# Attention and two feed-forward layers on one core: the second layer's weights converted after the attention, with three pair buffers and a new table of durations

## The chip, the core and the metric

The kernel runs on one core of a Trainium2 chip. The metric is the device time of one execution, in microseconds (us). Six queues work side by side: TensorE (PE) multiplies matrices, VectorE (DVE) and ScalarE (ACT) work on elements, GpSimd (POOL) does so more slowly, SyncE (SP) issues all transfers, and sixteen DMA engines move the data. Each queue runs its instructions strictly in the order in which they were written.

## The reference

Four batches of eight heads attend over 576 positions with a head size of 64, with a learned relative bias. The result goes through two feed-forward layers of width 2048 over 2304 tokens.

```python
scores = scale * np.matmul(q, k.transpose(0, 1, 3, 2))
h = np.maximum((psi_rel / psi_i)[..., None] @ w1 + b1, 0.0)
scores = scores + (h @ w2).transpose(2, 0, 1)[None]
attn = np.exp(scores - scores.max(-1, keepdims=True))
attn = attn / (attn.sum(-1, keepdims=True) + 1e-09)
x = heads_joined(np.matmul(attn, v))          # (2304, 512)
r = np.maximum(x @ w_in, 0.0)                 # first layer
x = (s * (r * r) + b) @ w_out
h = x @ moe2_w_in                             # second layer
return (h - np.tanh(h)) @ moe2_w_out
```

The attention's inputs are float32, and the four weight matrices of the layers are float64.

## The kernel before

**Precision.** Every operand of a matmul is held as a pair of float16 numbers, a high part and a low part that is what the high part left over. A product takes three matmuls (high by high, high by low, low by high). So the kernel spends much of DVE, ACT and POOL on making pairs: `copy_scale` makes the high part (DVE or ACT), `low_part` the low part (DVE). A float64 weight is first made float32 by three DVE instructions on its bits, `conv_steps` (L906, L909, L912), and squares of it are summed on ACT for the scale of the pair.

**Attention.** There are 144 units, each for 128 rows of scores of one head (or of two heads with 64 rows). A unit runs: scores on PE into `sp` (L747, four matmuls), bias and maximum on DVE (L761), exponential on ACT into `e` (L771), its high part into the pair buffer `hl` on ACT or DVE (L782, L780), its low part on POOL (L788), a DMA transposition of `hl` into `et` (L794), and the weighted sum on PE into `xp` (L807, L814, fourteen matmuls). Rings of buffers limit how many units are under way: two of `sp`, two of `e`, two of `hl`, four of `et`, four of the bias `bi`. Ahead of them the bias is computed in 36 steps: a hidden layer `hid` (L456 on DVE or L460 on ACT, four instructions a step), a matmul, and a copy to the DRAM tensor `btd`, from which each unit loads its rows.

**First layer.** Whenever 256 tokens have all their heads, a block of it can run: 192 matmuls into `ph` (L1203), relu and square on ACT, high part on DVE (L1226), low part on POOL (L1230), 192 matmuls into `po` (L1270), and a store to the DRAM tensor `x2d`. Nine blocks make 3456 matmuls of 256 columns. The inputs of the blocks lie in a ring `xt` of two.

**Second layer.** Five blocks of tokens run `pg` (L1499), tanh and difference, and `pq` (L1546), 960 matmuls each, nearly all of 512 columns. Its weights are 8 tiles of 128 by 2048. While the attention runs, `w2_tasks` brings each in four quarters through two staging places in `w1big`: load of 512 KB float64, three DVE steps of 512 columns, a square on ACT (L1324), and a store of the float32 values to the DRAM tensor `w2d`. When all squares are summed and the scale is known, tiles 0 and 1 are loaded again and split into pairs during the attention's end. The task `turn` then gives up the attention's memory, and tiles 2 to 7 are loaded from `w2d` (`w2x`) and split.

**Order.** The order on every queue is not written out. Each step is a task with a duration for each engine that may run it, dependencies, a priority, and the buffers that it takes. A planner (`Schedule.forward`) goes through time, starts at each moment the task of least priority value that could start, and writes the instructions in that order. So the durations and the constants at the head of the file decide the order of all queues and which of two engines gets a task.

Of the kernel before, what the change touches and what calls it, by code (L numbers as in the profile page):

```python
# [11 lines left out]
U32 = mybir.dt.uint32  # L12
# [13 lines left out]
SHARE0, QP, QA, SCU = 0, 9, 15, 29  # L26
T0, R0, T1, RU = 46.51, 2.21, 135.37, 2.75
QL0, QLEAD, QSTEP = 12.97, -15.94, 0.15
WI0, WI1, WO0, WO1 = 33.65, 103.52, 57.73, 120.8
W2A, W2B, W2U, W2V = 467.42, 815.12, 71, 7  # L30
AHEAD = 1.46
# [138 lines left out]
def tile_kernel(  # L170
# [36 lines left out]
    xt_p = ctx.enter_context(tc.tile_pool(name="xt", bufs=2))  # L207
# [96 lines left out]
    w2d32 = dram.tile([128, 8, 2048], F32, name="w2d32")  # L304
# [10 lines left out]
    ROWS = dict(bi=4, e=2, hl=2, et=4)  # L315
    hr = wp.tile([128, 8 * 2 * S], F16, name="hr")
# [129 lines left out]
    def hid(Q, t, eng):  # L446
        if Q < QA:
            i = (Q % 2) * 4 + t
            h = hr[:, i * 2 * S:(i + 1) * 2 * S].bitcast(F32)
# [5 lines left out]
        if eng == DVE:  # L455
# [16 lines left out]
    def bias_tasks(Q):  # L472
# [3 lines left out]
        for t in range(4):  # L476
# [3 lines left out]
            else:  # L480
# [3 lines left out]
                {DVE: 0.48, ACT: 0.70}, lambda e, Q=Q, t=t: hid(Q, t, e), deps, d, [hid_i[Q, t]] if Q >= QA else []  # L484
# [5 lines left out]
        if Q < QP:  # L490
# [6 lines left out]
            t_bmm[Q].append(sc.add({PE: 1.2}, mm, hs, d - 1000, [i], hi))  # L497
# [3 lines left out]
            t_ev.append(sc.add({ACT: 0.65, DVE: 0.70}, out, t_bmm[Q], d, [ev], [i]))  # L501
        else:
            for hf in range(2):
# [4 lines left out]
                t_bmm[Q].append(sc.add({PE: 0.6}, mm, hs + t_bmm[Q], d - 1000, [i], hi))  # L508
# [927 lines left out]
    for n in range(32):  # L1436
        w2_tasks(n)
# [203 lines left out]
```

## Time and profile before

| | us |
|---|---|
| three timed runs | 1154.21, 1153.5, 1149.24 |
| their median | 1153.5 |
| the profiled execution | 1156.14 |
| its span, first to last instruction | 1154.3 |

The span is 1.84 us shorter than the time of the same execution. In the profile a line such as L1203 is a line of the kernel before. "Busy" is the union of an engine's instruction times. Matmuls overlap each other, so a busy PE may still be slower than it could be. PEclk is the granted TensorE clock as a share of 2.4 GHz, and the DMA share is the mean busy share of the sixteen engines; overlapping packets can lift it above 1.

### The profile page before, as it was taken

The numbers are of one execution on the slowest core, as the hardware profiler recorded it, in microseconds if no ns is written. First come the engines' busy times: TensorE is split into PE (matmuls) and PEld (weight loads), VectorE is DVE, ScalarE is ACT, GpSimd is POOL, SyncE is SP. The second block draws the span as 40 slices with busy tenths as digits, with TensorE's granted clock in tenths as the row PEclk, the third lists the DMA queues.
The fourth block names the chain that finished last, engine by engine and source line by source line (L and its number), as shares of the span: only waits on it lengthen the run. The fifth ranks groups of instructions, "written<-read, shape, count | busy, mean of one in ns | idle before, by whom it ended". The sixth has DMA issues, their size and how long they took to land.

```text
span 1154.3 us, 23401 instructions
## 1 busy us (share of the span) xinstructions
PE 1031.2 (89%) x9024; PEld 696.4 (60%) x9024; DVE 804.6 (70%) x1704; ACT 575.1 (50%) x1114; POOL 330.4 (29%) x364
## 2 busy tenths in 40 slices
PE   4466589999988888989888899999999999999998
PEld 2233267776777677877777778888554444444443
DVE  7999999787666897888878764787755444344320
ACT  7987877776688674655546553342211111111110
POOL 0043255455454374554635443210000000000000
PEclk9566778999999899999999999999999999999999
DMA  9997884997999989999999993550001000000000
GB/s 337 321 294 172 245 227 94 199 202 172 219 247 234 257 189 243 243 228 231 225 209 243 205 187 82 177 198 31 21 10 46 10 19 10 19 10 10 19 19 27
DMA packets 268736, 176.96 MB, mean 153 GB/s; under 512 B 200528, under 2 KB 227792, under 8 KB 267856
## 3 DMA queue, kind: packets, MB, share of 16 engines
q1 hardware_dynamic: 268624, 175.47, 61.5%
q8 instruction: 70, 1.15, 0.4%
q14 instruction: 42, 0.34, 0.1%
HBM read 99.79 MB, written 28.44 MB: 111 GB/s over the span
## 4 chain that ended last, share of the span: by engine, by line
PE 54%; DMA 14%; DVE 12%; ACT 4%; issue 3%; POOL 1%; SPq 1%; DVEq 0%; ACTq 0%; POOLq 0%
PE pq L1546 16%; PE pg L1499 16%; DMA et<-hl 11%; PE po L1270 8%; PE ph L1203 6%; PE sp L747 3%; DVE sp L761 2%; PE pb L464 2%; PE xp L807 2%; POOL hl L788 1%; PE xp L814 1%; DVE w1big L909 1%; DVE hr L1226 1%; ACT e L771 1%; DVE w1big L912 1%
## 5 line engine op out<-in xcount | busy, mean ns | idle before, releaser
L788 POOL TENSOR_TENSOR hl<-e,hl 128x64 f16<-128x64 f32 (+1 forms) x288 | 236.3, 842 | 318.5 <-ACT hl L782 216.7
L1270 PE MATMUL po<-hr,w1big 128*128 128x256 f16 x1728 | 209.3, 277 | 7.3 <-DVE x L1284 3.8
L1203 PE MATMUL ph<-xt,w1big 128*128 128x256 f16 x1728 | 205.7, 275 | 0.2 <-DVE p2a L228 0.2
L1270 PEld LDWEIGHTS <-w1big 128*128 128x128 f16 x1728 | 168.2, 100 | 37.6 <-issue 8.3
L1203 PEld LDWEIGHTS <-w1big 128*128 128x128 f16 x1728 | 166.9, 99 | 27.9 <-issue 5.8
L1507 ACT ACTIVATE t<-pg,ich 128x512 f32<-128x512 f32 (+1 forms) x80 | 51.6, 645 | 243.8 <-PE pg L1499 243.8
L1511 DVE SCALAR_TENSOR_TENSOR t<-pg,ich,t 128x512 f32<-128x512 f32 (+1 forms) x80 | 55.7, 696 | 153.3 <-ACT t L1507 153.3
L1546 PEld LDWEIGHTS <-w2big 128*128 128x128 f16 x960 | 93.9, 98 | 94.2
L771 ACT ACTIVATE e<-sp,mx 128x576 f32<-128x576 f32 x144 | 105.6, 734 | 64.4 <-POOL hl L788 56.7
L761 DVE CUSTOM_DVE_ANT_0 sp<-sp,bi 128x576 f32<-128x576 f32 x144 | 109.4, 760 | 31.4 <-PE sp L747 20.0
L1546 PE MATMUL pq<-w1big,w2big 128*128 128x512 f16 x576 | 130.8, 379 | 0.0
L1230 POOL TENSOR_TENSOR hr<-r,hr 128x512 f16<-128x512 f32 x72 | 94.9, 1318 | 110.8 <-DVE hr L1226 95.7
L747 PE MATMUL sp<-ks,qs 128*128 128x288 f16 (+1 forms) x640 | 102.6, 303 | 26.5 <-ACT e L771 26.3
L807 PE MATMUL xp<-vp,et 128*128 128x64 f16 (+1 forms) x1440 | 66.1, 199 | 36.3 <-DMA et<-hl 33.2
L807 PEld LDWEIGHTS <-et 128*128 128x128 f16 (+1 forms) x1440 | 56.1, 104 | 61.3 <-DMA et<-hl 50.2
L1499 PE MATMUL pg<-hr,w2big 128*128 128x512 f16 x384 | 88.1, 379 | 0.0
L747 PEld LDWEIGHTS <-qs 128*128 128x128 f16 (+1 forms) x640 | 54.6, 104 | 52.2 <-issue 38.6
L1499 PE MATMUL pg<-hr,w1big 128*128 128x512 f16 x384 | 85.7, 379 | 0.0
L782 ACT ACTIVATE hl<-e 128x576 f16<-128x576 f32 x89 | 60.2, 679 | 41.5 <-DMA et<-hl 36.1
L1499 PEld LDWEIGHTS <-w1big 128*128 128x128 f16 x480 | 47.0, 98 | 45.9
L1499 PEld LDWEIGHTS <-w2big 128*128 128x128 f16 x480 | 46.9, 98 | 44.7
L1546 PE MATMUL pq<-w2big 128*128 128x256 f16 (+1 forms) x384 | 66.0, 326 | 0.0
(155 smaller groups left out, 1356.3 us busy)
## 6 DMA issues: line engine op xcount, KB each, us to landing
bi<-btd SPq DMA_DIRECT2D x72, 288.0 KB, 4.3
btd<-et SPq DMA_DIRECT2D x36, 288.0 KB, 3.6
qst<-in_qd SPq DMA_DIRECT2D x36, 256.0 KB, 4.7
w1big<-in_win SPq DMA_DIRECT2D x8, 1024.0 KB, 7.8
w1big<-in_wout SPq DMA_DIRECT2D x8, 1024.0 KB, 6.5
w1big<-in_win SPq DMA_DIRECT2D x16, 512.0 KB, 4.9
w2d<-w1big SPq DMA_DIRECT2D x32, 256.0 KB, 3.4
w1big<-in_wout SPq DMA_DIRECT2D x16, 512.0 KB, 5.3
```

The source lines that it names most:

```text
L747: nc.tensor.matmul(out=s_[r0:r0 + r, hf, 0:HS], lhsT=qs.tile[:, s, c * r:c * r + r], rhs=ks.tile[:, a, hf * HS:(hf + 1) * HS], start=s == ...
L761: nc.vector.tensor_tensor_reduce(out=st, in0=st, in1=bi.tile.rearrange("p (a b) -> p a b", a=2), scale=-1.0 / KAP, scalar=3.0e38, op0=ALU. ...
L771: nc.scalar.activation(out=put(e, row_tile("e")).rearrange("p (a b) -> p a b", a=2), in_=sp.tile[:, :, 0:HS], func=AF.Exp, scale=-1.0, bia ...
L782: nc.scalar.activation(out=h[:, 0:S], in_=e.tile, func=AF.Copy)
L788: nc.gpsimd.tensor_tensor(out=hl.tile[:, o:o + m], in0=e.tile[:, c:c + m], in1=hl.tile[:, c:c + m], op=ALU.subtract)
L807: nc.tensor.matmul(out=xp[r0:r0 + r, col:col + 64], lhsT=et.tile[:, n, r0:r0 + r], rhs=vp.tile[:, 0, n % 5, 64 * a:64 * a + 64], start=n = ...
L1203: nc.tensor.matmul(out=ph.tile[:, fi, :], lhsT=win_ap(1, sw, m, f), rhs=xa(sx, m), start=m == 0 and j == 0, stop=m == KM - 1 and j == 2,)
L1230: nc.gpsimd.tensor_tensor(out=rh[:, :, 1, :], in0=r.tile, in1=rh[:, :, 0, :], op=ALU.subtract)
L1270: nc.tensor.matmul(out=po.tile[:, :NB1], lhsT=wout_ap(1, sw, f, c), rhs=rhl[f // 8][:, f % 8, sr, :], start=f == 0 and j == 0, stop=f == K ...
L1499: nc.tensor.matmul(out=pg.tile[:, :n], lhsT=win_ap(2, sw, m, f), rhs=xh[:, sx, m, :n], start=m == 0 and i == 0, stop=m == KM - 1 and i == 2,)
L1511: nc.vector.scalar_tensor_tensor(out=tt.tile[:, :n], in0=pg.tile[:, :n], scalar=xs2[j][1], in1=tt.tile[:, :n], op0=ALU.mult, op1=ALU.subtract,
L1546: nc.tensor.matmul(out=pq.tile[:, :n], lhsT=wout_ap(2, sw, f, c), rhs=g[:, sr, :n], start=f == 0 and i == 0, stop=f == KF - 1 and i == 2,)
```

## The change

The weights of the second layer are no longer touched while the attention runs. The DRAM copy `w2d` is gone, and `turn` waits for the attention alone. After it, `w2_tasks(i, j)` loads half a tile (1 MB float64) into one of two `xr` buffers, converts it in steps of 1024 columns straight into a float32 place in the freed memory, and squares it. `w2_norm(g)` makes the scale of four tiles as soon as those four are in, so tiles 0 to 3 need not wait for 4 to 7. `w2_part(i, j)` splits from the float32 place. The ring `hl` grows to three buffers and the ring of first-layer inputs `xt` to four. POOL may run `hid` for the first seven bias steps. The two batches now alternate from the first group on (`SHARE0`), so that two units in a row use one bias tile. All durations given to the planner and all constants at the head are new.

```diff
-SHARE0, QP, QA, SCU = 0, 9, 15, 29
-T0, R0, T1, RU = 46.51, 2.21, 135.37, 2.75
+SHARE0, QP, QA, SCU, QG = 31, 8, 19, 48, 7
+T0, R0, T1, RU = 58.44, 2.06, 98.62, 3.64
...
-    w2d32 = dram.tile([128, 8, 2048], F32, name="w2d32")
...
-    ROWS = dict(bi=4, e=2, hl=2, et=4)
+    ROWS = dict(bi=4, e=2, hl=3, et=4)
...
-                {DVE: 0.48, ACT: 0.70}, lambda e, Q=Q, t=t: hid(Q, t, e), deps, d, [hid_i[Q, t]] if Q >= QA else []
+                {DVE: 0.45, ACT: 0.67, **({POOL: 1.5} if Q < QG else {})}, lambda e, Q=Q, t=t: hid(Q, t, e), deps, d, [hid_i[Q, t]] if Q >= QA else []
...
-        t_tr[u] = sc.add({SP: (0.62, 1.01)}, tr, [t_lo], d + 5 - 500, [et], [hl])
+        t_tr[u] = sc.add({SP: (0.62, 1.87)}, tr, [t_lo], d + 5 - 500, [et], [hl])
...
+    def w2_f32(i):
+        return (big2[0][:, i + 1, :] if i < 7 else w1big[:, 5, :]).bitcast(F32)
+
+    def w2_tasks(i, j):
+
+        raw = inst("xr")
+        prio = 1e3 + 20 * i + 10 * j
+        out = lambda: w2_f32(i)[:, j * 1024:(j + 1) * 1024]
...
+        t = load(to, w_src(win2, wout2, i, 2 * j, 2 * j + 2), 3.17 if f64 else 1.6, [t_turn], prio, [raw])
         if f64:
+            for m in range(3):
+                t = sc.add(
+                    {DVE: (0.75, 1.26, 1.2)[m]}, lambda _, m=m: conv_steps(raw.tile.bitcast(U32), out())[m](_),
+                    [t] + (staged if i == 7 else []), prio, [], [raw],
+                )
...
+    def w2_part(i, j, prio):
+        o = j * 1024
+        src = lambda: w2_f32(i)[:, o:o + 1024]
+        part = lambda s: w_pair(2, i)[:, s, o:o + 1024]
+        c = lambda: w2s["c", i // 4]
+        deps = [t_w2c[i // 4]] + (t_w2p[i - 1] if i % 4 else [])
+        th = sc.add({ACT: 1.04, DVE: 0.72}, lambda e: copy_scale(part(0), src(), c(), e), deps, prio)
+        tl = sc.add({DVE: 1.25}, lambda _: low_part(part(1), src(), c(), part(0)), [th], prio + 0.5)
...
-    goal += [x for i in range(2) for x in t_w2p[i]] + t_prep[0]
```

What the planner makes of it is read from the order of the built instructions. On SP, in the second half of the attention, the kernel before has loads of second-layer weights and stores to `w2d` between the transpositions of the units:

```order
L217 DMA qst<-in_qd 128x4x128
L794 DMA_TRANSPOSE et<-hl 128x9x128
L217 DMA w2d_85<-w1big 128x512 x2
L794 DMA_TRANSPOSE et<-hl 128x9x128
L217 DMA w1big<-in_win 128x1024 x2
L794 DMA_TRANSPOSE et<-hl 128x9x128
L873 DMA_TRANSPOSE xt<-xh 128x4x128
```

On SP at the end of the attention of the changed kernel, the last transpositions of units (`et`) and of layer inputs (`xt_own`) stand ahead of the first load of raw weights:

```order
L796 DMA_TRANSPOSE et<-hl 128x9x128
L886 DMA_TRANSPOSE xt_own<-xh 128x4x64 x2
L215 DMA w2raw<-in_win 128x2x1024 x4
L215 DMA x2d<-x_10167 128x256
L215 DMA x2d<-x_10225 128x256
L215 DMA w2raw<-in_win 128x2x1024 x2
```

All sixteen raw loads now follow the last transposition, and none lies among the units.

On DVE, in the attention's last units, the kernel before converts weights (L906, L909, L912) between the bias steps of two units (the rows `sp,mx`):

```order
L761 ISA sp,mx<-sp,bi 128x2x288
L761 ISA mx 128x1
L765 TENSOR_SCALAR mx<-mx 128x1
L906 TENSOR_SCALAR w1big<-w1big 128x512
L909 SCALAR_TENSOR_TENSOR w1big<-w1big 128x512
L912 SCALAR_TENSOR_TENSOR w1big<-w1big 128x512
L1226 CAST hr<-r 128x2x256
L761 ISA sp,mx<-sp,bi 128x2x288
```

On DVE behind the last unit of the changed kernel, the same conversion, twice as wide, stands between the high parts (`hr`) and the results (`x`) of the last blocks of the first layer:

```order
L918 TENSOR_SCALAR w2big<-w2raw 128x1024
L921 SCALAR_TENSOR_TENSOR w2big<-w2raw,w2big 128x1024
L1244 CAST hr<-r 128x2x256
L924 SCALAR_TENSOR_TENSOR w2big<-w2raw,w2big 128x1024
L918 TENSOR_SCALAR w2big<-w2raw 128x1024
L1244 CAST hr<-r 128x2x256
L921 SCALAR_TENSOR_TENSOR w2big<-w2raw,w2big 128x1024
L924 SCALAR_TENSOR_TENSOR w2big<-w2raw,w2big 128x1024
L1303 TENSOR_SCALAR x_10167<-po,esc,bcol 128x128 x2
```

The conversion moved from between the units to behind all of them, among first-layer blocks that moved with it.

At the start of POOL's queue in the changed kernel, seven `hid` instructions of the bias stand where the kernel before has its first low parts of `hl`:

```order
L454 TENSOR_SCALAR hr<-u_sb,cst_sb 128x576
L454 TENSOR_SCALAR xt_own<-u_sb,cst_sb 128x576
L454 TENSOR_SCALAR hr<-u_sb,cst_sb 128x576 x5
L790 TENSOR_TENSOR hl<-e,hl 128x64
L790 TENSOR_TENSOR hl<-e,hl 128x512
```

These seven were DVE's or ACT's before.

## Rows read from the trace of the kernel before

**Rows 1.** Stages: us, busy of each engine (x instructions), PEclk, DMA share, GB/s.

```profile
0.00:146.00 146.00, 81.78 (x620) 39.05 (x621) 132.85 (x258) 122.14 (x209) 34.74 (x38) 0.71 0.91 272
...
200.00:300.00 100.00, 96.70 (x1130) 71.95 (x1127) 77.31 (x202) 73.73 (x148) 48.06 (x59) 1.00 0.84 189
300.00:424.00 124.00, 110.03 (x1299) 89.08 (x1300) 91.15 (x232) 92.99 (x200) 59.12 (x68) 0.97 1.07 242
424.00:706.00 282.00, 253.87 (x2903) 213.12 (x2901) 224.43 (x521) 155.04 (x349) 144.86 (x164) 0.99 0.97 213
706.00:782.00 76.00, 72.17 (x659) 64.11 (x657) 58.80 (x114) 27.46 (x45) 13.95 (x10) 1.00 0.48 160
782.00:1154.00 372.00, 368.47 (x1878) 183.41 (x1875) 167.35 (x295) 62.56 (x96) 0.00 (x0) 1.00 0.06 19
```

**Rows 2.** Stages, exponentials alone (L771 on ACT, two rows a unit).

```profile
200.00:300.00 100.00, 20.32 (x50) 1.00 0.84 189
...
424.00:706.00 282.00, 52.98 (x128) 0.99 0.97 213
```

**Rows 3.** Stages, first layer's L1203 alone: PE, then weight loads.

```profile
424.00:706.00 282.00, 93.22 (x797) 76.37 (x795) 0.99 0.97 213
706.00:782.00 76.00, 23.64 (x216) 20.81 (x213) 1.00 0.48 160
```

**Rows 4.** The same for the first layer's L1270.

```profile
424.00:706.00 282.00, 93.69 (x768) 75.34 (x768) 0.99 0.97 213
706.00:782.00 76.00, 43.70 (x384) 37.37 (x384) 1.00 0.48 160
```

**Rows 5.** Chain that ended last, two pieces: start, length, engine and line.

```profile
732.68 18.35 PE ph L1203 x168
...
867.88 10.36 PE pg L1499 x48
```

**Rows 6.** Timeline, us 596 to 616: start, length, engine, operation, idle before and releaser.

```profile
598.07 0.69 ACT L782 ACTIVATE hl<-e 128x576 f16<-128x576 f32 x1
...
600.02 0.65 PE L747 MATMUL sp<-ks,qs 128*128 128x288 f16 x4
...
601.12 2.79 PE L1270 MATMUL po<-hr,w1big 128*128 128x256 f16 x24
...
602.10 1.36 SPq L794 DMA_TRANSPOSE et<-hl  x1
...
607.25 0.68 ACT L782 ACTIVATE hl<-e 128x576 f16<-128x576 f32 x1 [1.25 <-DMA et<-hl]
```

**Rows 7.** Groups by shape, us 424 to 706: busy us, mean ns, idle before.

```profile
L788 POOL TENSOR_TENSOR hl<-e,hl 128x512 f16<-128x512 f32 x65 | 81.0, 1247 | 0.0
...
L912 DVE SCALAR_TENSOR_TENSOR w1big<-w1big 128x512 uint32<-128x512 uint32 x32 | 29.0, 906 | 0.6
L909 DVE SCALAR_TENSOR_TENSOR w1big<-w1big 128x512 uint32<-128x512 uint32 x31 | 25.6, 825 | 0.8
...
L906 DVE TENSOR_SCALAR w1big<-w1big 128x512 uint32<-128x512 uint32 x31 | 19.4, 624 | 5.1 <-DMA w1big<-in_win 4.2 <-DMA w1big<-in_wout 0.8
```

**Rows 8.** Groups by shape, whole span.

```profile
L909 DVE SCALAR_TENSOR_TENSOR w1big<-w1big 128x1024 uint32<-128x1024 uint32 x16 | 21.3, 1330 | 0.5
...
L364 DVE SCALAR_TENSOR_TENSOR w2big<-w2x,w_c,w2big 128x1024 f16<-128x1024 f32 x12 | 18.1, 1547 | 0.1
...
L456 DVE TENSOR_SCALAR hr<-u_sb,cst_sb 128x576 f32<-128x576 f32 x21 | 9.5, 513 | 0.0
```

**Rows 9.** Waits, us 424 to 706: us in total, times, longest.

```profile
ACT hl L782 <- DMA et<-hl: 19.4, 17, 2.5
PE xp L807 <- DMA et<-hl: 16.1, 15, 2.4
```

**Rows 10.** DMA issues, us 424 to 706: count, KB each, median us to landing.

```profile
w2d<-w1big SPq DMA_DIRECT2D x32, 256.0 KB, 3.4
...
et<-hl SPq DMA_TRANSPOSE x66, 4.5
```

More of the change, by code (lines that the diff above doesn't have):

```diff
@@ L454, in hid @@
         col = pt_sb[:, 4 * Q + t:4 * Q + t + 1]
-        if eng == DVE:
+        if eng == POOL:
+            nc.gpsimd.tensor_scalar(
+                out=h, in0=u_sb[:, st:st + S], scalar1=col, scalar2=0.0, op0=ALU.add, op1=ALU.max
+            )
+        elif eng == DVE:
             nc.vector.tensor_scalar(
@@ L513, in out @@
                     evac(Q, ev.tile[:, hf * HS:(hf + 1) * HS], i.tile[:, 0:HS], e)
-                t_ev.append(sc.add({ACT: 0.41, DVE: 0.42}, out, t_bmm[Q] + t_ev, d, [] if hf else [ev], [i, ev]))
+                t_ev.append(sc.add({ACT: 0.40, DVE: 0.44}, out, t_bmm[Q] + t_ev, d, [] if hf else [ev], [i, ev]))
         t_bw[Q] = load(
-            btd[it][128 * (Q % 8):128 * (Q % 8) + 128, :], lambda: ev.tile, 0.82, t_ev, d, uses=[ev]
+            btd[it][128 * (Q % 8):128 * (Q % 8) + 128, :], lambda: ev.tile, 0.93, t_ev, d, uses=[ev]
         )
@@ L678, in v_tasks @@
         us = [st] if st else []
-        th = sc.add({ACT: 0.78, DVE: 0.50}, hi, deps, due - 4, [vp], us)
+        th = sc.add({ACT: 0.72, DVE: 0.50}, hi, deps, due - 4, [vp], us)
         tl = sc.add(
@@ L752, in unit_tasks @@
         t_qkm[u] = sc.add(
-            {PE: 0.5 if full else 0.58}, qk, t_klo[b, p] + t_khi[b, p] + [t_qlo[n], t_qkm.get(u - 1)] + first, d - 1000, [sp],
+            {PE: 0.56 if full else 0.64}, qk, t_klo[b, p] + t_khi[b, p] + [t_qlo[n], t_qkm.get(u - 1)] + first, d - 1000, [sp],
             [ks, qs],
@@ L818, in unit_tasks @@
         t_pv[u] = sc.add(
-            {PE: 0.42 if full else 0.78}, pv, [t_tr[u], t_vlo[b, p], t_pv.get(u - 1)], d + 10 - 1000,
+            {PE: 0.58 if full else 0.9}, pv, [t_tr[u], t_vlo[b, p], t_pv.get(u - 1)], d + 10 - 1000,
             [xp_i] if p == 0 else [], [et, vp, xp_i],
@@ L827, in tile_kernel, with xt_tile @@
     ]
+    xt_n = [0]
+    def xt_tile():
+        i = xt_n[0] % 4
+        xt_n[0] += 1
+        t = xt_own[:, i] if i < 2 else w1big[:, 4, (i - 2) * 2048:(i - 1) * 2048]
+        return t.rearrange("p (a n) -> p a n", a=8)
     def x_tasks(n):
@@ L891, in tile_kernel @@
     W32 = [0, 1, 2, 3, 2, 3, 4, 5]
+    t_conv_all = {i: [] for i in range(8)}
     t_wld, t_conv, t_wsq, t_whi, t_wlo = {}, {}, {}, {}, {}
@@ L944, in w1_split @@
             sc.add(
[L945 removed]
+                {DVE: 1.25},
                 lambda _, j=j: low_part(
@@ L1293, in moe1_tasks @@
             m = len(rng)
-            t_evac[n] = sc.add({ACT: 0.17 * m + 0.28, DVE: 0.14 * m + 0.30}, out, last + [t_es], ready - 400, [x2], [po])
+            t_evac[n] = sc.add({ACT: 0.3 * m + 0.1, DVE: 0.3 * m + 0.05}, out, last + [t_es], ready - 400, [x2], [po])
             t_x2w[n].append(load(
@@ L1346, in tile_kernel @@
-    t_w2p = {}
-    def w2_part(i, o, src, n, deps, prio, uses=()):
-        pr = w_pair(2, i) if i < 2 else None
-        def part(s):
-            return w_pair(2, i)[:, s, o:o + n]
-        c = lambda: w2s["c"][:, i // 4:i // 4 + 1]
-        th = sc.add(
-            {ACT: 0.06 + 0.9e-3 * n, DVE: 0.06 + 0.59e-3 * n}, lambda e: copy_scale(part(0), src(), c(), e), deps, prio,
-            [], uses,
-        )
-        tl = sc.add(
-            {DVE: 0.08 + 1.1e-3 * n}, lambda _: low_part(part(1), src(), c(), part(0)), [th], prio + 0.5, [], uses
-        )
+    t_w2sq, t_w2c = {}, {}
@@ L1558, in out @@
                 nc.scalar.activation(out=oo.tile[:, :n], in_=pq.tile[:, :n], func=AF.Copy, scale=xs2[j][3])
-            t = sc.add({ACT: 0.1 + 1e-3 * n}, out, t_o[j][-1:], 0, [oo], [pq])
+            t = sc.add({ACT: 0.1 + 1e-3 * n}, out, t_o[j][-1:] + [t_osc[j]], 0, [oo], [pq])
             load(
```

228 lines of the change are left out of this document (109 added, 119 removed).

## The prediction

> **What bounds the kernel now.** I read the stages first [rows 1]. They are three kernels in one. Up to 146 us DVE is busy 132.85 us and PE waits for it, at a mean clock of 0.71. From 782 us on PE is busy 368.47 of 372 us and nothing else matters. Between them the attention and the first layer share PE. There PE is the busiest engine (96.70 of 100 us, then 253.87 of 282 us), and the DMA share is 0.84 to 1.07.
>
> What is lost in the middle is seen by costing PE's work at full pace. A matmul of 256 columns takes 18.35/168 = 0.109 us, one of 512 columns 10.36/48 = 0.216 us [rows 5]. A unit, four score matmuls and fourteen of a weighted sum, takes 601.12 - 600.02 = 1.10 us [rows 6]. From 424 us to the attention's end at 706 us there are 64 units [rows 2] and 797 + 768 = 1565 first-layer matmuls [rows 3, 4]: 70 + 171 = 241 us of work in 282. So 41 us are lost there, 13 us inside busy time (253.87 against 241, a factor of 1.052) and 28 us idle (10%).
>
> The timeline shows what sets the pace of a unit [rows 6]. The high part at 598.07 takes one of two `hl` buffers. Its transposition is issued at 602.10, since SP is in order and has other transfers ahead, and lands 4.5 us later in the median [rows 10]. The next high part but one starts at 607.25, after a wait of 1.25 us for just that DMA. So two buffers were held 9.2 us, which allows a unit each 4.6 us; the stage's mean is 282/64 = 4.4. Downstream this shows as waits for the transposition, 19.4 us on ACT and 16.1 us on PE [rows 9].
>
> **The change part by part.** I divide the span at unit 80 (424 us) and at the last weighted sum (706 us). How PE's work is spread over the pieces I count in the order of its queue. The first-layer matmuls ahead of unit 80 are 1248 before and 1296 now. From there to the last weighted sum they are 1608 and 1068. Behind it are 600 and 1092. So 492 matmuls, 54 us, move from the attention to its end: nothing is gained unless the attention gets shorter by more than that.
>
> *Up to unit 80.* The second layer's weights are not touched here in either kernel, and DVE's order up to unit 30 holds the same work but for some `hid`. Seven of these go to POOL, 7 x 0.513 = 3.6 us off a saturated DVE [rows 8]. POOL's own price for them has no row. The nearest is its subtraction of 512 columns, 1.247 us [rows 7], so they hold POOL for some 9 us, while POOL is busy only 34.74 of 146 us [rows 1]. If DVE stood still for all of these, the head would lose 9 - 3.6 = 5 us. The row says that this is possible: two-input steps of 512 columns take 0.825 and 0.906 us where POOL is busy half the time [rows 7], and 1.33 us for twice the width in the head [rows 8].
>
> The Trainium skill, page SBUF — State Buffer, section Who interferes with whom, states that a DVE instruction with two inputs in SBUF, or in a two-port mode, and a GpSimd instruction that reads SBUF block one another for the whole instruction. By that rule the head would end up to 5 us later than with the seven left where they were, and the whole at 1133; no row has POOL and DVE on `hid` together.
>
> With `SHARE0` the first sixteen units load eight bias tiles instead of sixteen. The third `hl` buffer takes away waits which, at the later stage's 16.1 us for 64 units on PE, would be at most 13 us for the 53 units from 200 to 424 us. The 48 extra matmuls cost 5 us. I take 6 us less in all: 418 us, with bounds 411 and 431.
>
> *From unit 80 to the last weighted sum.* Removed from DVE: 29.0 + 25.6 + 19.4 = 74 us of conversion in 94 instructions [rows 7], from ACT the squares, from the DMA 32 loads of 512 KB (twice a store's 256 KB) and 32 stores [rows 10], about 24 MB of the 213 x 282 = 60 MB moved [rows 1]. DVE at 224.43 of 282 us was not the bound, so its 74 us are no direct gain; they make bias steps and high parts start on time. The DMA did 0.97 x 282 = 274 us of work. By bytes the weights are 40% of it, 110 us; at the head's pace (272 GB/s at a share of 0.91, so 299) they are 80 us. So 164 to 194 us stay. SP also loses these 64 issues, which stood ahead of transpositions.
>
> PE keeps 1068 matmuls by the order; the trace has 1565 of the 1608 after 424 us, so I take 1040: 113 + 70 = 184 us. Times 1.052 for the loss inside busy time it is 193 us. For idle time I have two rows: 3.3% in the stage 200 to 300 us with its DMA share of 0.84, and 10% in the present stage. They give 200 and 215 us. I take 206, since the DMA share would be 0.80 to 0.94, between those rows. That is 3.2 us a unit. Three `hl` buffers held 9.2 us allow 3.07; two would allow 4.6, so the third buffer is what makes this possible at all. Bounds: 193, no idle time, and 64 x 3.7 = 237, should a unit get only part of the way from 4.4.
>
> *From the last weighted sum to the end.* Before, 1154.3 - 706 = 448 us with 600 first-layer matmuls [rows 3, 4], 65.5 us; the second layer and its losses are the other 383. Now 1092 matmuls, 119 us, so 502 us if the weights arrive under cover. The cover is these 119 us and 12 us of `pg`, 131 us, until PE reaches the first `pq`. DVE must do in it 16 conversions of about 0.7 + 2 x 1.33 us, 54 us, and 16 low parts of 1.547 us, 25 us [rows 8], and I estimate 50 us of high parts, scales and block 0's differences from the order's count. That is about 130 of 131 us plus what the last units give, some 10 us. It is full but it fits, as scales for tiles 0 to 3 are made first. The 64 small stores and 14 reloads of `w2d` are gone too, but ACT's squares return: they lie beside PE. I add 3 us for slips, with bounds of -5 and +25. So 505 us.
>
> Sum: 418 + 206 + 505 = 1129 us of span, and 1131 with the 1.84 us outside it. The profiled execution took 1156.1, 2.6 above the median of three; taking the same 25 us off the median of 1153.5 gives 1128.
>
> **The rivals.** *The attention sheds work and no time.* If the attention from unit 80 on takes 228 us, 3.6 us a unit, the 54 us moved behind it eat the gain: 418 + 228 + 505 + 2 gives 1153. For it speaks that a unit's chain of exponential, high part, low part and transposition stays, with two `e` buffers and one SP queue. Against it: the buffer that was waited for [rows 9] is the one that is added. The Trainium skill has a rule for it in Perfetto Trace Analysis, section Optimization Strategy: where the busiest engine changes over time, interleaving the regimes may help, and this change separates two. By that rule the time would stay near 1153 or rise; the rows so far bear it out only in part, as DMA and buffers, which interleaving loads too, are what is waited for.
>
> *The pace stays at the 4.0 us a unit of the stage from 200 to 300 us* (25 units in 100 us [rows 2], without any of these weights). Then 64 units take 256 us and the kernel ends at 418 + 256 + 505 + 2 = 1181, slower than before; every 0.1 us a unit is 6.4 us, and from 3.7 on it is slower. The place would be the exponential of unit u waiting for POOL's low part of unit u - 2. Against it: in that stage PE was busy 96.70 of 100 us, so PE set that pace, with bias matmuls and 18 of the first layer a unit; now it has 16 and no bias.
>
> *DVE becomes the bound behind the attention.* Its work of 130 us has to be done in some 141. Were it idle for a quarter of that, waiting for raw loads through two buffers, the last pair would be ready 25 us late: 418 + 206 + 502 + 25 + 2 gives 1153. This adds to either of the others.
>
> **How the numbers follow.** The forecast, 1106 to 1147, has a chance of 0.63, and 0.07 lies below it. No gain, 1148 to 1159, has 0.15, fed by the first and third rival. Slower has 0.15, most of it the pace rival. A measurement of this kernel can tell about 0.5% from no change, 6 us, so faster is 0.70, same 0.15, slower 0.15. The range of 1106 to 1162 leaves out 0.07 below and some 0.12 above.
>
> **What would show it.** Right: the last weighted sum at 615 to 635 us, units at about 3.2 us from unit 80 on, ACT's wait for the transposition of `hl` nearly gone, PE without a gap of more than a few us between there and the first `pq`. Wrong: a last weighted sum after 650, PE idle before the first `pg` or `pq`, or unit 16 later than in the kernel before.

## The result, and the profile after

The changed kernel takes 1134.67 us (1130.3 to 1135.39, 4 runs) against 1152.06 us (1149.24 to 1154.21, 4 runs) for the kernel before: a ratio of 0.9843, with a 95% interval of 0.9807 to 0.9878. It is faster by 17 us, 1.6%, where 25 were forecast. The profiled execution has a span of 1133.6 us; that of before had 1154.3.

Stages of the changed kernel, with the columns of [rows 1]; the attention now ends near 623 us instead of 706.

```profile
0.00:146.00 146.00, 84.54 (x668) 39.02 (x672) 128.81 (x247) 123.63 (x210) 47.56 (x43) 0.72 0.86 254
...
200.00:300.00 100.00, 94.47 (x1138) 69.73 (x1135) 83.79 (x210) 66.29 (x145) 51.33 (x62) 0.94 0.88 194
300.00:424.00 124.00, 116.65 (x1398) 99.23 (x1395) 93.23 (x233) 86.89 (x191) 61.13 (x69) 1.00 1.07 223
424.00:632.00 208.00, 200.70 (x2454) 169.26 (x2454) 150.17 (x419) 120.14 (x263) 126.18 (x153) 1.00 0.97 179
632.00:760.00 128.00, 123.45 (x1127) 109.98 (x1125) 105.15 (x153) 64.56 (x139) 29.76 (x20) 1.00 0.46 156
```

From 424 to 632 us PE is busy 96% of the time, where it was 90% from 424 to 706 us [rows 1]. The DMA share there has stayed at 0.97, though fewer bytes move (179 GB/s, not 213).

The three pieces into which the prediction cut the span: up to unit 80, to the last weighted sum, to the end.

```profile
0.00:426.00 426.00, 339.56 (x3639) 238.95 (x3643) 359.95 (x777) 324.01 (x625) 190.54 (x200) 0.87 0.90 220
426.00:623.00 197.00, 190.09 (x2359) 159.99 (x2359) 144.24 (x402) 113.82 (x252) 120.96 (x150) 1.00 0.99 180
623.00:1133.00 510.00, 497.08 (x3027) 296.85 (x3025) 281.79 (x465) 131.17 (x240) 32.98 (x23) 0.99 0.17 56
```

Length less PE's busy time is PE's idle time. PE's whole work is the same in both kernels (1031.2 us busy before, 1026.7 after), so this is the account to keep: 86.4, 6.9 and 12.9 us idle here; 87.3, 28.1 and 7.4 us before, cut at 424 and 706 us. The attention lost 21 us of idle time, the end gained 5.5, and the first 424 us, where most of it lies, kept theirs. That makes 17 of the 21 us by which the span is shorter. The other 4 are busy time, which for the same matmuls lies anywhere from 1021.5 to 1032.7 us in the runs below, but for e1: a few us between two kernels can come from there.

Waits of the changed kernel in its attention, 426 to 623 us (us in total, times, longest), and the landing of the transposition there (count, median us), beside [rows 9, 10]:

```profile
ACT e L773 <- POOL hl L790: 35.5, 30, 3.9
...
DVE hl L782 <- DMA et<-hl: 12.3, 9, 2.4
ACT hl L784 <- DMA et<-hl: 10.8, 10, 2.6
...
PE xp L809 <- DMA et<-hl: 3.2, 7, 1.1
PE sp L749 <- ACT e L773: 3.0, 5, 1.2
```

```profile
et<-hl SPq DMA_TRANSPOSE x65, 4.1
```

Three more waits of the kernel before, 424 to 706 us:

```profile
ACT e L771 <- POOL hl L788: 43.9, 40, 2.9
...
PE sp L747 <- ACT e L771: 7.1, 10, 1.5
DVE hl L780 <- DMA et<-hl: 5.7, 3, 2.6
```

What has nearly gone is PE's own wait for the transposition: 3.2 us instead of 16.1 [rows 9]. The wait for a pair buffer has not gone. It is halved on ACT (19.4 to 10.8 us) and doubled on DVE (5.7 to 12.3), together 25.1 us before and 23.1 now. The exponential waits for POOL's low part, the place that the pace rival named, and it did so before (43.9 us, now 35.5). Little of this reaches PE: it waits 3.0 us for exponentials, and waited 7.1.

The chain of the changed kernel where PE stands still, behind the attention (start, length, engine and line):

```profile
760.08 2.48 DVE w2big L362 x2
762.56 0.68 DVE w2big L357
763.26 2.48 DVE w2big L362 x2
765.74 0.41 DVE t L1529
766.19 11.56 PE pg L1517 x84
```

PE has its one long gap before the last of these, 4.54 us. The 84 matmuls behind it take 11.56 us, where 84 x 0.109 [rows 5] would be 9.2: the clock granted from 760 to 780 us is 0.83, so part of that stretch ran at 1.2 GHz.

### The profile page after: what moved, and what is told of

The parts are those of the page before. It is cut to its first block, busy times and chain, and to the rows that moved or that the text cites. A ratio compares the mean times of both kernels' runs of the same rounds, so it can differ in the third digit from the quotient of the medians.

```text
span 1133.6 us, 23200 instructions
## 1 busy us (share of the span) xinstructions
PE 1026.7 (91%) x9023; PEld 695.8 (61%) x9026; DVE 786.0 (69%) x1642; ACT 569.0 (50%) x1116; POOL 344.5 (30%) x371
## 4 chain that ended last, share of the span: by engine, by line
PE 60%; DVE 20%; DMA 7%; ACT 5%; issue 4%; POOL 2%; SPq 1%; DVEq 0%; ACTq 0%; POOLq 0%
PE pq L1564 16%; PE pg L1517 16%; PE po L1289 10%; PE ph L1221 8%; DMA et<-hl 5%; PE sp L749 3%; PE pb L466 3%; DVE sp L763 2%; PE xp L809 2%; DVE ks L362 1%; PE xp L816 1%; DVE w1big L921 1%; ACT e L773 1%; DVE vp L362 1%; DVE hr L1244 1%
## 5 line engine op out<-in xcount | busy, mean ns | idle before, releaser
L790 POOL TENSOR_TENSOR hl<-e,hl 128x64 f16<-128x64 f32 (+1 forms) x288 | 232.2, 829 | 229.9 <-ACT hl L784 82.9
L1289 PE MATMUL po<-hr,w1big 128*128 128x256 f16 x1728 | 204.6, 273 | 6.9 <-ACT x L1308 4.3
L1564 PE MATMUL pq<-w1big,w2big 128*128 128x512 f16 (+1 forms) x960 | 195.3, 358 | 0.0
L1289 PEld LDWEIGHTS <-w1big 128*128 128x128 f16 x1728 | 165.8, 98 | 33.6 <-issue 8.3
L1221 PEld LDWEIGHTS <-w1big 128*128 128x128 f16 x1728 | 166.9, 98 | 31.1 <-issue 10.1
L1517 PE MATMUL pg<-hr,w2big 128*128 128x512 f16 x768 | 173.6, 379 | 0.0
L1517 PEld LDWEIGHTS <-w2big 128*128 128x128 f16 x960 | 95.0, 99 | 96.7 <-issue 4.7
L1564 PEld LDWEIGHTS <-w2big 128*128 128x128 f16 x960 | 93.9, 98 | 94.0
L1221 PE MATMUL ph<-xt_own,w1big 128*128 128x256 f16 x960 | 113.8, 274 | 4.4 <-ACT et L359 2.6
L1221 PE MATMUL ph<-w1big 128*128 128x256 f16 x768 | 88.2, 273 | 0.3 <-DVE na L1180 0.3
L466 PE MATMUL pb<-hr,cst_sb 128*32 128x288 f32 x268 | 41.2, 589 | 28.4 <-DVE et L357 10.9
L1234 ACT ACTIVATE r<-ph 128x512 f32<-128x512 f32 x72 | 42.6, 591 | 40.2 <-PE ph L1221 38.5
```

The costliest lines, as they stand in the source:

```text
L466: nc.tensor.matmul(out=pb[32 * t:32 * t + 32, 0:HS], lhsT=w2d_sb, rhs=hid_t[Q, t][:, hf * HS:(hf + 1) * HS], start=True, stop=True,)
L790: nc.gpsimd.tensor_tensor(out=hl.tile[:, o:o + m], in0=e.tile[:, c:c + m], in1=hl.tile[:, c:c + m], op=ALU.subtract)
L1221: nc.tensor.matmul(out=ph.tile[:, fi, :], lhsT=win_ap(1, sw, m, f), rhs=xa(sx, m), start=m == 0 and j == 0, stop=m == KM - 1 and j == 2,)
L1289: nc.tensor.matmul(out=po.tile[:, :NB1], lhsT=wout_ap(1, sw, f, c), rhs=rhl[f // 8][:, f % 8, sr, :], start=f == 0 and j == 0, stop=f == K ...
L1517: nc.tensor.matmul(out=pg.tile[:, :n], lhsT=win_ap(2, sw, m, f), rhs=xh[:, sx, m, :n], start=m == 0 and i == 0, stop=m == KM - 1 and i == 2,)
L1564: nc.tensor.matmul(out=pq.tile[:, :n], lhsT=wout_ap(2, sw, f, c), rhs=g[:, sr, :n], start=f == 0 and i == 0, stop=f == KF - 1 and i == 2,)
```

## The experiments

Each run is compared with the kernel before on the same chip, which took 1155 to 1156.5 us there. PE's idle time in the profiled runs, worked out as above (length of the piece: idle us), with the first-layer matmuls that stand behind the last weighted sum in PE's queue:

| kernel | ratio to before | to unit 80 | to last weighted sum | to the end | matmuls behind |
|---|---|---|---|---|---|
| before | 1 | 424: 87.3 | 282: 28.1 | 448: 7.4 | 600 |
| after | 0.9843 | 426: 86.4 | 197: 6.9 | 510: 12.9 | 1092 |
| e1 after, two pair buffers | 1.0433 | 458: 99.6 | 255: 11.3 | 496: 50.0 | 516 |
| e2 before, three pair buffers | 1.0158 | 420: 103.4 | 242: 28.7 | 508: 10.2 | 1116 |
| e3 after, hidden rows on DVE | 0.9749 | 419: 81.4 | 197: 5.9 | 511: 13.8 | 1092 |
| e4 after, conversion in two steps | 0.9785 | 425: 88.3 | 195: 6.1 | 509: 12.3 | 1092 |
| e5 before, no conversion steps | 0.9902 | 424: 88.8 | 269: 17.4 | 449: 7.7 | 600 |
| e6 before, no loads either | 0.9810 | 424: 92.7 | 258: 8.8 | 448: 6.7 | 600 |
| e7 after, highs on ACT | 0.9808 | 422: 85.1 | 194: 4.7 | 513: 13.8 | 1092 |
| e8 after, numbers of before | 1.0120 | 450: 104.9 | 205: 11.2 | 510: 21.2 | 996 |
| e9 after, two x blocks | 1.0058 | 425: 87.7 | 195: 7.4 | 541: 33.2 | 1104 |
| e10 e3 with late halves | 0.9761 | 418: 79.3 | 196: 6.1 | 509: 12.5 | 1092 |
| e11 e2 without loads, conversion | 0.9956 | 424: 104.4 | 218: 11.5 | 508: 9.9 | 1116 |
| e12 after, planned without POOL rows | 0.9927 | 411: 96.9 | 201: 8.6 | 531: 16.0 | 1248 |

### What the weights cost in the attention: e5 and e6

```diff
 # e5, in w2_tasks of the kernel before
-t = sc.add({DVE: (0.40, 0.66, 0.66)[m]}, f, ...)
+t = sc.add({DVE: (0.40, 0.66, 0.66)[m]}, f if n < 2 else lambda _: None, ...)
 # e6, besides: the load of piece n is issued for n < 2 only
```

> The kernel before with the three VectorE steps of the second layer's conversion left out for 30 of its 32 pieces (90 instructions, some 71 us of VectorE beside the attention; the second layer then works on wrong weights); loads, squares, stores and the order of all else stay. Theory one (VectorE's conversion did not hold the attention, the two pair buffers and the queues did): the last weighted sum stays within 6 us of 705 and the time within 5 us of the kernel before. Theory two (VectorE's share was in the way): the last weighted sum comes 10 to 30 us earlier and the time is 8 to 25 us shorter.

> As the run without the conversion's steps, and 30 of the 32 loads of the second layer's weights (512 KB each, 15.7 MB) left out too; the stores of the converted copy and their reading back stay. Against that run: theory one (the loads in the queues make the transpositions land late): TensorE's wait for the transposition behind unit 80 falls by half or more, and the time by another 5 to 15 us. Theory two (two pair buffers set the pace, whatever the queues do): within 4 us of that run.

e5 took 1144.29 us (0.9902, 0.9878 to 0.9925), e6 1132.98 us (0.981, 0.9782 to 0.9837). From unit 80 to the last weighted sum, first e5, then e6 (columns of [rows 1]), then e6's landing of the transposition and the wait for it:

```profile
424.00:693.00 269.00, 251.65 (x2889) 212.46 (x2888) 161.22 (x429) 153.47 (x347) 135.38 (x164) 0.99 0.99 224
```

```profile
424.00:682.00 258.00, 249.24 (x2893) 212.50 (x2892) 161.11 (x430) 153.35 (x348) 136.50 (x165) 0.99 0.84 173
```

```profile
et<-hl SPq DMA_TRANSPOSE x66, 3.7
...
PE xp L807 <- DMA et<-hl: 5.4, 6, 1.7
```

Theory two of e5 holds: DVE's conversion steps cost 12 us although DVE was busy only 224.43 of 282 us [rows 1]. Theory one of e6 holds: the loads cost another 11 us. With them gone the transpositions land in 3.7 us instead of 4.7 in e5 (4.5 before [rows 10]), and PE's wait for them falls from 14.3 us in e5 (16.1 before [rows 9]) to 5.4. What e5 took from PE were other waits: those for exponentials fell from 7.1 to 2.8 us, and those for results of DVE, 4.7 us before, are gone. So 19 of the 28 idle us of the attention came from these two, 11 and 9 us, and they go with two pair buffers: 258 / 64 = 4.0 us a unit, with PE busy 97% of the time. The account does not cover all of e6's gain: its span is 24 us shorter, of which 15 are idle time (5 came back ahead of unit 80) and 9 busy time. The changed kernel, which moves this work, takes nearly as long as one in which most of it isn't done (0.9843 and 0.981 of before).

### What the third pair buffer does: e1, e2 and e11

```diff
 # e1, in the changed kernel
-ROWS = dict(bi=4, e=2, hl=3, et=4)
+ROWS = dict(bi=4, e=2, hl=2, et=4)
-("hl", 3)
+("hl", 2)
 # e2, in the kernel before
-ROWS = dict(bi=4, e=2, hl=2, et=4)
+ROWS = dict(bi=4, e=2, hl=3, et=4)
-("hl", 2)
+("hl", 3)
-hr = wp.tile([128, 8 * 2 * S], F16, name="hr")
+hr = wp.tile([128, 2 * CH], F16, name="hr")
 # hid: rows with Q odd and t == 3 in the staging ring
 # e11: e2 with the edits of e6
```

> The changed kernel with two pair buffers for the low and high half of the exponentials instead of three, the order planned anew for two. Theory (the third buffer sets the pace of the attention): a buffer is held some 9 us, so two allow 4.6 us a unit where the changed kernel took 3.1; the stretch from unit 80 to the last weighted sum, 197 us with three, becomes 230 to 270, ScalarE's wait for the transposition out of the pair buffer in it comes back to 15 us or more (10.8 with three), and the time is 1145 to 1170. Rival (the conversion that left the attention made the pace, since transpositions now land sooner): the stretch stays at 195 to 212 and the time at 1130 to 1140.

> The kernel before with a third pair buffer; its bytes come from the table of hidden rows, whose eighth slot (every second quarter-block's last row) goes through the staging ring instead. The second layer's weights are still converted beside the attention and written to DRAM. Theory (the third buffer sets the pace): TensorE's 28 us of idle time from unit 80 on falls to 15 or less, and the time is 1132 to 1144. Rival (the conversion beside the attention holds VectorE and the queues, and a third buffer finds nothing to do): the idle time stays at 22 to 30 us and the time at 1147 to 1156.

> The kernel before with the third pair buffer and without 30 of 32 loads and conversions of the second layer's weights: the fourth corner beside before (1156), the third buffer alone (1173) and the loads and conversions alone left out (1133). Theory (the third buffer by itself shifts first-layer work behind the attention, 1116 matmuls against 600, and the idle time ahead of unit 80 that comes with the new order stays; only the wait for the transpositions goes): 1145 to 1158, slower than with two buffers and the same work left out. Rival (with the queues free the third buffer is worth its own 10 us or more): 1132 or less.

e1 took 1207.07 us (1.0433, 1.0406 to 1.046), e2 1173.05 us (1.0158, 1.0129 to 1.0186), e11 1150.09 us (0.9956, 0.9937 to 0.9974). The theory on e1 and e2 falls, and so does its rival on e1, while the rival on e2 has the idle time right and the time wrong: the third buffer alone makes the kernel before slower, and without it the changed kernel is far slower than either. e1 from its last weighted sum on (stage, then waits of PE up to 900 us, then the worst 20 us):

```profile
713.00:1209.00 496.00, 446.04 (x2474) 243.67 (x2467) 271.75 (x455) 107.04 (x196) 12.45 (x8) 0.96 0.16 56
```

```profile
PE pg L1517 <- DVE t L1529: 19.8, 3, 11.4
PE psum L423 <- DVE s2w L1367: 6.2, 1, 6.2
```

```profile
780.00:800.00 20.00, 6.76 (x36) 4.53 (x36) 18.45 (x29) 4.53 (x6) 0.00 (x0) 0.68 0.15 53
```

In e1 the attention takes the 255 us expected from unit 80 on, but PE idles only 11.3 of these, and ACT's wait for the transposition is 7.2 us (DVE's 8.7), not 15 or more: the plan with two buffers fills the longer attention with first-layer work, and 516 matmuls are left behind it, 56 us at 0.109 us [rows 5], to cover DVE's conversion. DVE is busy 18.45 of 20 us there and PE waits: 50.0 us idle, part of it at a mean clock of 0.68. This is the third rival, DVE as the bound behind the attention, at one and a half times its price (37 us more idle than in the changed kernel, for 25), from a cause that it did not have: too little cover. The span is 75 us longer than the changed kernel's. Of the other 38 us, 13 are idle ahead of unit 80, 4 in the attention, and 21 are busy time (1048.1 us against 1026.7), at a granted clock of 0.96 behind the attention, where the changed kernel has 0.99. PE's wait for the transposition in e1's attention, with two buffers:

```profile
PE xp L809 <- DMA et<-hl: 1.5, 2, 0.9
```

e2's attention, its stretch from unit 80 on and PE's wait in it:

```profile
420.00:662.00 242.00, 213.27 (x2525) 177.54 (x2524) 199.06 (x472) 142.17 (x319) 136.94 (x153) 0.98 1.06 227
```

```profile
PE xp L809 <- DMA et<-hl: 19.0, 13, 3.3
```

It is 40 us shorter than before, at an unchanged 28.7 us of idle time: 516 matmuls have only moved behind it. The wait for the transposition is still there, 19.0 us, with the weights' loads in the queues. As its theory said, e11 takes that away (5.9 us), but like e2 it idles some 17 us more up to unit 80 than the kernel before, and it is slower than e6 by as much as e2 is slower than before (1.5 and 1.6%). Whether that comes from the new plan or from the rows that I put through the staging ring these runs can't tell.

So in none of the three pairs does the third buffer shorten PE's wait for the transposition: 16.1 and 19.0 us in the kernel before, 5.4 and 5.9 without loads and conversion, 1.5 and 3.2 in the changed structure. PE's idle time in the attention goes from 28.1 to 28.7, from 8.8 to 11.5, and from 11.3 to 6.9. What the buffer does is in the plan: units go through quickly (3.1 us each, where e1 and e6 take 4.0), first-layer work stays behind, and this is cover. Without it the changed kernel is 68 us slower (e1 against after: 5.9% of 1152). That is not the price of the buffer alone: e1 keeps the numbers at the head of the file, chosen for three buffers, and what two would cost with numbers of their own no run shows.

### Four x blocks: e9

```diff
-("xt", 4)
+("xt", 2)
-i = xt_n[0] % 4
+i = xt_n[0] % 2
```

> The changed kernel with two x blocks instead of four, planned anew. In the order that comes out, 1104 of the first layer's matmuls stand behind the last weighted sum (1092 with four blocks). Theory (the blocks are of no weight; what lets the first layer's work lag is the attention's own pace): 1131 to 1139. Rival (with two blocks the transposition of x waits for the first layer, and the attention behind it): last weighted sum after 635, time 1145 or more.

It took 1161.63 us (1.0058, 1.0037 to 1.0079). The rival's time came, 1145 us or more, but not its place: the last weighted sum comes at 620.0 us, as with four blocks. SP's queue there, first e9 with its longest wait, then the changed kernel:

```profile
614.00 1.29 SPq L796 DMA_TRANSPOSE et<-hl  x1
635.40 5.38 SPq L884 DMA_TRANSPOSE xt_own<-xh  x3
```

```profile
SPq L884 <- PE ph L1221: 20.7, 1, 20.7
```

```profile
624.54 2.46 SPq L886 DMA_TRANSPOSE xt_own<-xh  x2
627.16 0.98 SPq L215 DMA_DIRECT2D w2raw<-in_win  x2
```

In e9 no transposition is issued for 20 us: that at 635.40 goes to a buffer that an older block still held, and the chain shows `ph` x144, the first layer's reading, from 620.20 to 636.03. The loads of the weights stand behind the last transposition of x, so they begin at 648.7 instead of 627.2 us. The conversion is 20 us late (first step at 654.5, not 634.4) and PE idles 33.2 us behind the attention. The blocks set the date at which the conversion may begin; the count of matmuls behind, 1104, did not show that. Here too the numbers at the head stayed those of the full change.

### The head: e3, e8 and e12

```diff
 # e3, in hid
-nc.gpsimd.tensor_scalar(
+nc.vector.tensor_scalar(
 # e12
-SHARE0, QP, QA, SCU, QG = 31, 8, 19, 48, 7
+SHARE0, QP, QA, SCU, QG = 31, 8, 19, 48, 0
 # e8: that line and the four below it as in the kernel before, QG = 0
```

> The changed kernel with its seven hidden rows of GpSimd issued on VectorE at the same places of the program; the order on every other engine is the same. Theory (the rows on GpSimd, 2.2 to 2.7 us each, held TensorE's bias products, and slowed VectorE's own rows from 513 to 649 ns): the first exponential at 47 to 51 us instead of 55, unit 16 at 141 to 146 instead of 148.8, VectorE's rows back at 510 to 530 ns, and the end 3 to 7 us earlier, 1126 to 1131. Rival one (the order of the head, not GpSimd, made it late): first exponential at 53 or later, time 1132 to 1137. Rival two (the head comes earlier, but is waited for again before unit 80): unit 0 earlier by 4 or more, unit 80 at 424 to 427 and the time 1131 to 1136.

> The changed kernel with the option of hidden rows on GpSimd taken from the planner, which then orders the whole program anew (1248 first-layer matmuls behind the last weighted sum instead of 1092). Theory (the rows on GpSimd cost what the run with the same order showed): first exponential at 51 or before, 1122 to 1130. Rival (the planner's other numbers were chosen with these rows, and a new order loses more than the rows cost): 1135 or more.

> The changed kernel with the numbers of the planner's table (start dates, lead times, how far ahead the transfers are issued) set back to those of before, no hidden rows on GpSimd; buffers, blocks, the place of the conversion and the durations in the code are the changed kernel's. Theory (the buffers and the conversion's place carry the gain): 1128 to 1145, and the first exponential back at 46 to 50 us. Rival (the numbers belong to the structure, and without them the order does not fit): 1150 or more.

e3 took 1126.19 us (0.9749, 0.973 to 0.9767): the theory holds, with the first exponential at 51.1 us (0.1 past its range), unit 16 at 142.6, unit 80 at 419.0 instead of 425.8. The 7 us stay to the end of the span (1127.1). DVE's rows up to 60 us by shape (busy, mean ns of one), the changed kernel and then e3, and the changed kernel's again by their length (least, median and most ns):

```profile
L458 DVE TENSOR_SCALAR hr<-u_sb,cst_sb 128x576 f32<-128x576 f32 x13 | 7.8, 649 | 1.5 <-PE pb L466 1.5
```

```profile
L458 DVE TENSOR_SCALAR hr<-u_sb,cst_sb 128x576 f32<-128x576 f32 x13 | 6.3, 515 | 0.0
```

```profile
L458 DVE TENSOR_SCALAR hr<-u_sb,cst_sb x13: 505/521/1001, 5.7 to 21.6; 128x576 f32<-128x576 f32 x13
```

The changed kernel's timeline at its start, two rows of POOL and DVE's beside them, and who waited for line 454 in all (us, times):

```profile
5.76 2.75 POOL L454 TENSOR_SCALAR hr<-u_sb,cst_sb 128x576 f32<-128x576 f32 x1 [5.32 <-DVE u_sb L431]
8.49 2.20 POOL L454 TENSOR_SCALAR xt_own<-u_sb,cst_sb 128x576 f32<-128x576 f32 x1
```

```profile
5.70 2.30 DVE L458 TENSOR_SCALAR hr<-u_sb,cst_sb 128x576 f32<-128x576 f32 x4
10.77 0.82 DVE L357 TENSOR_SCALAR et<-pb,cst_sb 128x576 f32<-128x576 f32 x1 [2.78 <-PE pb L466]
```

```profile
  PEld pb L466: 7.9, 5
  PE pb L466: 4.2, 4
```

Seven rows cost POOL some 17 us and spared DVE 3.6. The mean of 649 ns hides two kinds of row: of the sixteen that DVE has beside these seven (the thirteen above and three into `xt_own`), ten take 0.51 to 0.52 us as without them, and six take 0.70 to 1.00. PE's bias products wait for the POOL rows, and with PE the queue behind.

e8 took 1168.25 us (1.012, 1.0082 to 1.0158), the rival's side: with the numbers of before the new structure loses all that it won and 1.2% more. The first exponential comes at 39.6 us, ahead of the theory's 46 to 50, and unit 16 only at 162.7; 18 us more idle time lie ahead of unit 80, 8 behind the attention. `SHARE0` is among these numbers, so the run does not part the order from the shared bias tiles.

e12 took 1146.67 us (0.9927, 0.9903 to 0.9951), the rival's side again, and it shows best what misleads here: unit 16 comes at 122.4 us (148.8 in the changed kernel), unit 80 at 411.4 and the last weighted sum at 611.9, all earlier, and the end is 9 us later (span 1143.0). Waits of PE in e12 from unit 16 to 300 us, and its last piece:

```profile
PE sp L749 <- ACT e L773: 22.6, 13, 4.5
```

```profile
612.00:1143.00 531.00, 515.02 (x3188) 312.16 (x3186) 285.29 (x482) 131.72 (x238) 35.14 (x24) 0.99 0.16 54
```

The units ran ahead of the first layer, and PE, with less of its work left for these gaps, waited for exponentials (22.6 us; from unit 16 to 300 us the changed kernel waits 3.3). Up to unit 80 it idles 10 us more, and the 156 matmuls more (17 us) are done at the end.

### The gap behind the attention: e4, e7 and e10

```diff
 # e4, in w2_tasks
-conv_steps(raw.tile.bitcast(U32), out())[m](_)
+conv_steps(raw.tile.bitcast(U32), out())[m](_) if m < 2 else None
 # e7, in w2_part
-th = sc.add({ACT: 1.04, DVE: 0.72}, ...)
+th = sc.add({ACT: 1.04}, ...)
 # e10: e3, and
-w2_part(i, j, 1e3 + 80 * (i // 4) + 70 + 2 * i)
+w2_part(i, j, (1e3 + 70 if i < 4 else 9e3) + 2 * i)
```

> The changed kernel with the third of three steps in the conversion of the second layer's weights left out (its 16 instructions on VectorE, 1.2 us each, some 19 us in all; the lowest bits of these weights are then missing); the order of all else is the same. Theory (behind the attention VectorE is the chain, and TensorE's one gap of 4.5 us before the second layer's eighth product group of the first block is all that it costs): the gap is gone, and the time is 3.5 to 6 us shorter, 1127 to 1131. Rival (something else is late at the same point, the loads or the squares on ScalarE): the gap stays at 2 us or more and the time at 1132 to 1136.

> The changed kernel with the 16 high halves of the second layer's weights always on ScalarE (the planner had put most on VectorE, 0.68 us each), GpSimd's hidden rows left as they are. Leaving out 19 us of VectorE's conversion had not closed TensorE's gap of 4.5 us before the first block's eighth product group; the trace shows a block of 13 us of VectorE's weight halves in its queue ahead of the step that frees the product buffer. Theory (the order in VectorE's queue makes the gap): with the highs elsewhere and the steps interleaved, the gap is under 1 us and the time 3 to 5 us under the changed kernel's 1134.7. Rival (the gap moves to the next block or to the outputs): 1133 to 1137.

(The first words of this label don't apply: POOL's rows stay.)

> The changed kernel with its seven hidden rows of GpSimd on VectorE (as in the run that did this alone, 1126 us) and the weight halves of the second layer's second matrix ranked behind the steps that free the product buffers. Theory (the 4.5 us gap was the order of VectorE's queue, and only that): no gap over 1 us behind the attention, 1120 to 1124. Rival (VectorE has too much to do there in any order, as when ScalarE took the highs and the waits turned up at the output products): 1125 to 1130.

e4 took 1130.49 us (0.9785, 0.9766 to 0.9804), which would pass for the theory. The trace says otherwise: the gap is still 3.9 us, and 2.4 of the 4.5 us that the span is shorter were there at unit 16, ahead of the edit. DVE's queue in e4 before the step that frees the product buffer (the step at 761.98):

```profile
748.17 0.16 DVE L226 TENSOR_SCALAR p2a<-psum 128x1 f32<-128x1 f32 x1 [0.40 <-PE psum L423]
...
749.85 2.48 DVE L362 SCALAR_TENSOR_TENSOR w2big<-w2big,w_c 128x1024 f16<-128x1024 f32 x2
...
759.58 2.48 DVE L362 SCALAR_TENSOR_TENSOR w2big<-w1big,w_c,w2big 128x1024 f16<-128x1024 f32 x2
761.98 0.48 DVE L1529 SCALAR_TENSOR_TENSOR t<-pg,ich,t 128x256 f32<-128x256 f32 x1
```

The scales of the last four tiles need a sum that stands in PE's queue; it ends at 748.1, and from there 13 us of halves stand in one block in DVE's queue. Work left out ahead of that only leaves DVE waiting for others: from the last weighted sum to the gap 20.8 us for ACT's squares and 8.5 for PE's results, where the changed kernel has 10.1 and 2.3. e7 and e10 break the block up, and the gap before `pg` goes; PE then waits for DVE at the output products (in total, times, longest), e7 first:

```profile
PE pq L1564 <- DVE w1big L1536: 2.5, 3, 1.7
...
PE pq L1564 <- DVE w2big L362: 1.2, 3, 0.4
```

```profile
PE pq L1564 <- DVE w2big L362: 3.4, 4, 1.7
```

e7 took 1133.88 us (0.9808, 0.9782 to 0.9835), no different from the changed kernel; e10 took 1127.9 us (0.9761, 0.9739 to 0.9784), no different from e3. Both rivals hold. PE waits for DVE there, some 3 to 5 us, in any of the three orders.

**A version faster than both** is e3: 0.9749 (0.973 to 0.9767) against the changed kernel's 0.9843 (0.9807 to 0.9878).

## Why the prediction was right, and where not

The sum was 418 + 206 + 505 = 1129 us of span and it came out as 425.8 + 196.7 + 511.1 = 1133.6.

**Up to unit 80** the step that failed is the price of the seven rows on POOL. I took 1.247 us from a subtraction to half-width output; a row takes 2.20 to 2.75 us. And I priced the time that it takes from DVE, at most 5 us, not the one that PE and the queues wait for it. With the rows back on DVE unit 80 comes at 419.0 us, the 418 of the forecast. That the other terms of this piece were right does not follow: no run parts the third buffer, the shared bias tiles and the added matmuls. By the rule of the Trainium skill (page SBUF — State Buffer, section Who interferes with whom) a DVE instruction and a POOL instruction on the shared port block each other for a whole instruction. The size that I gave by it, 5 us, was near the 7 us found by luck: what PE waits for is the POOL row, which takes 2.20 us even while DVE stands idle (8.49 us; DVE has no row from 8.00 to 10.77), 2.29 to 2.75 otherwise. If the rule covers these rows, the measurement differs from it: no DVE row waits for a whole POOL row, ten of sixteen keep their time beside one and six take 0.2 to 0.5 us longer. For the thirteen `hr` rows this is 13 x 0.134 = 1.7 us in all. What holds these six no run shows.

The third buffer's gain there, up to 13 us, is not to be seen as such: e3, without POOL's rows, idles 6 us less than before in this piece. The sign that I had set for wrong, a later unit 16, came (148.8 for 142.4 us).

**From unit 80 to the last weighted sum** I was 9 us too high, because I took 206 between the rows with 3.3% and 10% of idle time, on the ground that the DMA share would lie between them. The share stayed at 0.97 and PE idled 3.5%. Of the 9 us, 6 are idle time (13 in the sum, 6.9 measured) and 3 busy time (193 and 190.1). The mechanism beneath it is half wrong. Two buffers were to allow 4.6 us a unit, and e1 and e6 take 4.0 with PE busy, so their limit is 4.0 us or less, and no run shows it. That "the third buffer is what makes this possible at all" stands for the pace, 3.1 us, in so far as no run with two came near it, but not for the time: with two buffers, PE's idle time there goes when the weights' loads and steps go (e6), and of DVE's 74 us, which I called no direct gain, the steps were worth 12 us (e5).

**From the last weighted sum to the end** I was 6 us too low. The account by cover was the right one, but DVE was not as full as I had it: it was busy 115 of the 143 us from 623 to 766 us (105.15 of 128 in the row from 632 to 760 above). So its work was less than my 130 us and its idle time, which I priced only in a rival, was more; that the two nearly cancel is luck. The 3 us were the wrong slip: the gap is 4.5 us, and the slow clock behind it costs 2.4 more; 2 us I have not traced. DVE's waits in the changed kernel, 623 to 766 us:

```profile
DVE hr L1244 <- ACT r L1239: 10.1, 6, 2.8
DVE w2big L918 <- DMA w2raw<-in_win: 3.5, 4, 1.6
...
DVE w2big L918 <- DMA w2raw<-in_wout: 1.2, 1, 1.2
```

"Waiting for raw loads" is 4.7 us of it, not a quarter of the time; ACT's squares are more. What PE meets is the block of halves that stands behind a sum in its own queue (e4).

**The rivals** were real mechanisms of this kernel but tied to the wrong switches. An attention whose gain the moved work eats is what e2 shows: 40 us shorter, not an idle microsecond less, and the end 17 us later. DVE as the bound behind the attention is e1 and e9, where cover or start date is missing. The pace rival named a wait that is there, and was there before, at a wrong price: 35.5 us of waiting for POOL's low part leave PE 3.0 us of waiting for exponentials. The rule that I weighed from the Trainium skill (page Perfetto Trace Analysis, section Optimization Strategy), that regimes with different bounds may gain by interleaving, brings no gain for these weights: the kernel that separates them is 17 us faster. The interleaved loads and steps were in the way of what PE waited for, and leaving them out where they stood is worth 23 us (e6).

**The signs.** The last weighted sum at 622.5 us, 3.1 us a unit, and no long gap up to the first `pq` were signs of being right that came; the gap of 4.5 us comes behind that. ACT's wait for the transposition, 10.8 us, is not "nearly gone"; PE's is.

**What I did not price** decided most of the risk: without the x blocks 25 us are lost (e9 against after, 2.15% of 1152), without the retuned numbers 32 (e8). What the weights cost in the attention is shown by leaving them out (e5, e6). That the other parts keep the moved work covered is shown only with the planner's numbers left as they were chosen for all parts together (e1, e9), and what the shared bias tiles do alone no run shows.

## What to carry to other kernels

Keep the account in idle time of the engine that bounds the kernel, stretch by stretch: a faster pace of units only moves its work (e2, e12). Before work is moved beside other work, work out two things, how long the cover is and at what date the moved work may start; either can be lost by a change elsewhere (e1, e9). Leaving work out can look right and prove nothing: e4's 4 us were not at the gap. A small step given to an idle engine costs what the chain waits for it, not the time that it saves on the busy one (e3).

## What the runs showed of the hardware

A row of 576 FP32 values takes 0.51 us on DVE and 2.2 to 2.75 us on POOL, 4 to 5 times as long. With both at work on such rows, most DVE rows keep their time and six of sixteen take 0.2 to 0.5 us longer. Transpositions that share queues with 512 KB loads land in 4.7 us (e5), without these in 3.7 (e6), at a DMA share that falls only from 0.99 to 0.84. And gaps of a few us late in the program cost more than themselves: the clock granted was 0.83 around one of 4.5 us, and 0.68 in e1 where they came in a row; over the whole of e1 PE's busy time is 1048.1 us for the same work, 21 us more.
